# A running sum over the sequence: how its block totals reach the output

## The chip, the core and the metric

The kernel runs on one core of a Trainium2 chip. The core has five engines with queues of their own: TensorE (PE, with its weight loads as PEld) for matrix products, VectorE (DVE), ScalarE (ACT), GpSimd (POOL) and SyncE (SP), and 16 DMA engines that move data. SP, ACT and POOL can issue transfers. Work is held in SBUF (128 partitions); products land in PSUM. The metric is the device time of one execution in microseconds. Each engine works through its own queue in order and waits for other engines by semaphores.

## The reference

Two branches read the same x (2048 positions, 448 channels) and are mixed by a gate of one number per position:

```python
g = _sigmoid((x * gate_w).sum(-1, keepdims=True))
a = _A_ref(x, A_wqkv, A_wo)          # linear attention, 16 heads of 28
b = _B_ref(x, ...)                   # long convolution, plus x * D_skip
return g * a + (1 - g) * b
```

Branch A: q, k, v are products of x with a 448 x 1344 weight; phi(t) = t + 1 for positive t, else exp(t). Per head, kv is the sum over all positions of phi(k) times v, z the sum of phi(k); a position's output is phi(q) kv / (phi(q) z), and then a product with `wo`.

Branch B convolves each channel with a kernel K[d, l] = 2 Re(sum over n of C exp(A dt l)). For the inputs drawn here K hardly changes over the 2048 positions, so that the convolution is a running sum of x along the sequence times one number per channel (`near` in the kernel). The kernel tests this for each channel and has a full convolution (`general_conv`) behind a branch for inputs where it does not hold; the branch is not taken in these runs.

## The kernel before, in words

**Tiling.** Position s = 16 p + c lies on partition p in chunk c. So a chunk is 128 positions, one on each partition, and 16 chunks (NC) make up the sequence. The running sum then has two levels: along the 16 chunks on each partition, and over the totals of all earlier partitions. `y` (128 x 16 x 448) collects the running sum and x times D_skip.

**The running sum.** The rows of x lie once more in `wvo` (chunks 0 to 7) and `room` (chunks 8 to 15), four chunks being a group; `home(c)` is a chunk's row. `running(c)` (L428) adds a row to the PSUM sum and puts the sum, times `near`, back in the row. `skip(c)` (L251, POOL) writes x * D_skip to `y`. `group_add(g)` (L436) adds a group's four rows to `y` with one accumulating transfer that POOL issues. After chunk 15's row, that row holds each partition's total: `whole_split` (L439) splits it in a high part (ScalarE) and a low part (POOL), `whole_head` (L445) multiplies both with a triangle of ones on TensorE, which leaves in PSUM for each partition the totals of all before it. These have to be added to all 16 rows of `y`. ScalarE copies them to `over`, and `head_add(g)` (L451) adds `over` to a group's four rows of `y`, again with an accumulating transfer that POOL issues, with `over` read four times.

**The first loop** (L514, chunks 2 to 13) has per step c, in TensorE's order: the k product of chunk c+1 (11 matmuls, `project`), the q product of chunk c, and the products `do_g(c)` of phi(k) with x, which accumulate over all chunks in four PSUM tiles `g`. Around it `split_t` and `split_n` split the two layouts of x of chunk c+2 in high parts (ScalarE) and low parts (POOL); `k_feature`, `k_high` and `k_low` are phi of k, with the column sums of phi(k) in `zb`; `q_post` is phi of q, kept in `pq`, and the gate's exponential in `e1`. `gate(a, b)` (L398) turns `e1` into the gate's denominators and `og` (one minus the gate) for chunks a to b-1.

**Between the loops** (L666 to L787) chunk 14 is handled, the column sums of `zb` over the partitions are formed by a product with ones (`zo`), kv and `wo` are multiplied, and the first chunks of the last loop are prepared.

**The last loop** (L805) has per chunk: `norm_a` (POOL, phi(q) times z), `norm_b` (VectorE, sum per head), `norm_d` (reciprocal, with the gate), `norm_c` (POOL L613 and L619 and VectorE L616, phi(q) scaled, to two places in `room`), `turn` (four transposes on TensorE into `tr`, split by ScalarE and VectorE into `th`), `attend` (11 products into `a`), `final_b` (VectorE: `ot` = `og` * `y` + `a`, then the output transfer from one of two buffers) and `final_c` (a copy by ScalarE). `norm_c` works two chunks ahead of `attend`, `norm_a` six ahead. `late` (L788) puts phi(q) of chunk 15 into the steps 5 to 7.

The order on each engine is the order of the program, written out by hand. What matters around the change in the first loop's end:

- step 12: `whole_split` after `skip(14)`
- step 13: `whole_head` behind the k product of chunk 14; `group_add(3)` after `skip(15)`; the copy to `over` after `k_high`; `head_add(0)` and `head_add(1)` at the step's end
- after the loop: `gate(0, 14)`, and `gate(14, 15)` behind the copy of `zb`
- last loop: `head_add(2)` in step 2, `head_add(3)` in step 3, both behind `norm_c`

`norm_a` writes to three places in `room` (elements 1024 to 2367 of 3584), `norm_c` to two (0 to 1023).

Of the kernel before, what the change touches and what calls it, by code (L numbers as in the profile page):

```python
# [31 lines left out]
QA = 1  # L32
QW = 512
EDGE = 16
PADS = 352
G = 4
ROWS = {6: (0, 1), 7: (2, 3, 4), 8: (5, 6, 7), 9: (8, 9, 10), 10: (11, 12, 13), 11: (14, 15)}
SMALL = 2.0 ** -70
# [104 lines left out]
def gated_mix_kernel(ctx: ExitStack, tc: tile.TileContext, xin, wq_d, wvo_d, abc_d, ldt_d, dsk_d,  # L143
# [36 lines left out]
    room = const.tile([P, 2 * G, D], F32, name="room")  # L180
    over = const.tile([P, D], F32, name="over")
    near = const.tile([P, D + PADS], F32, name="near")[:, :D]
    rf = room.rearrange("p r d -> p (r d)")

    xp = work.enter_context(tc.tile_pool(name="xp", bufs=4))
# [52 lines left out]
    def split_t(c):  # L238
        w = xt[c] = xt_p.tile([P, 2 * NAT], F32R, name="xt", tag="t")
        ACT.copy(w[:, :NAT], turned[c])  # L240
        low(POOL, w[:, NAT:], turned[c], w[:, :NAT])
# [37 lines left out]
    def s4d_prepare():  # L279
        tt = lambda eng, o, a, b, op: eng.tensor_tensor(out=o, in0=a, in1=b, op=op)  # L280
        stt = lambda o, a, k, b, op1: DVE.scalar_tensor_tensor(out=o, in0=a, scalar=k, in1=b, op0=ALU.mult, op1=op1)
        junk = [yf[:DJ, F0 + (i - 2) * 2 * N:F0 + (i - 1) * 2 * N].rearrange("p (i n) -> p i n", i=2) for i in range(2)]
        s0, s1, am, pn, b0, n0, n1 = (small() for _ in range(7))
        o = ps.tile([P, 512], F32, name="sums", tag="v0")
        side.append(o)
        dt, p0, p1, d2, md, b1 = (o[:DJ, D + i * J:D + (i + 1) * J] for i in range(6))
        for j in range(J):
            ACT.activation(abc[0][:, 0, j], abc[0][:, 0, j], AF.Exp)
        ACT.activation(dt, ldt, AF.Exp)
        ACT.activation(d2, dt, AF.Square)  # L290
        yield
        for j in range(J):
            ACT.activation(junk[0], abc[0][:, :, j], AF.Square, accum_out=am[:, j:j + 1])
            ACT.activation(junk[0][:, 0], abc[1][:, 0, j], AF.Copy, accum_out=s0[:, j:j + 1])
            DVE.scalar_tensor_tensor(out=junk[1], in0=abc[1][:, :, j], scalar=1.0, in1=abc[0][:, :, j], op0=ALU.mult,
                                     op1=ALU.mult, accum_out=s1[:, j:j + 1])
            if j % 2:
                yield
        tt(DVE, md, am, d2, ALU.mult)
        stt(p0, s0, 2.0, dt, ALU.mult)  # L300
        stt(n0, s0, 2.0, dt, ALU.mult)
        stt(p1, s1, -2.0, d2, ALU.mult)
        stt(n1, s1, -2.0, d2, ALU.mult)
        DVE.tensor_scalar(out=md, in0=md, scalar1=SMALL, scalar2=None, op0=ALU.is_le)
        stt(b0, p0, -1.0, n0, ALU.max)
        stt(b1, p1, -1.0, n1, ALU.max)
        yield
        DVE.tensor_scalar(out=p0, in0=p0, scalar1=-BIG, scalar2=BIG, op0=ALU.max, op1=ALU.min)
        DVE.scalar_tensor_tensor(out=md, in0=b0, scalar=1.0 / FAR, in1=md, op0=ALU.is_ge, op1=ALU.mult)
        stt(okc, b1, FLAT, b0, ALU.is_le)  # L310
        DVE.scalar_tensor_tensor(out=md, in0=b0, scalar=FAR, in1=md, op0=ALU.is_le, op1=ALU.mult)
        tt(DVE, okc, okc, md, ALU.mult)
        tt(DVE, pn, p0, okc, ALU.mult)
        DVE.tensor_reduce(out=oks, in_=okc, op=ALU.add, axis=AX.X)
        yield
        o = ps.tile([P, 512], F32, name="p", tag="v1")
        for j in range(J):
            PE.transpose(o[:, j * DJ:(j + 1) * DJ], pn[:, j:j + 1].to_broadcast([DJ, P]), ident[:DJ, :DJ])
        ACT.copy(near, o[:, :D])
# [108 lines left out]
    def running(c):  # L428
        if not c:
            sums.append(ps.tile([P, 512], F32, name="r", tag="v0")[:, :D])  # L430
            ACT.copy(sums[0], home(0))
        else:
            DVE.tensor_tensor(out=sums[0], in0=home(c), in1=sums[0], op=ALU.add)
        DVE.tensor_tensor(out=home(c), in0=near, in1=sums[0], op=ALU.mult)

    def group_add(g):  # L436
        POOL.dma_start(out=y[:, g * G:(g + 1) * G], in_=homes[g // 2][:, g % 2 * G:][:, :G], accum_op=ALU.add)

    def whole_split():  # L439
        w = tp.tile([P, 2, D], F32R, name="sums", tag="v0", bufs=1)  # L440
        sums[0] = w
        ACT.copy(w[:, 0], home(NC - 1))
        low(POOL, w[:, 1], home(NC - 1), w[:, 0])

    def whole_head():  # L445
        o = ps.tile([P, 512], F32, name="v", tag="v0")[:, :D]
        for i in range(2):
            PE.matmul(o, lhsT=tri, rhs=sums[0][:, i], start=i == 0, stop=i == 1)
        sums[0] = o

    def head_add(g):  # L451
        POOL.dma_start(out=y[:, g * G:(g + 1) * G], in_=over[:, None, :].to_broadcast([P, G, D]), accum_op=ALU.add)

    prep = s4d_prepare()
    def steps(n):
        for _ in range(n):
# [49 lines left out]
    def split_o(j):  # L506
        w = xn_p.tile([P, NX], F32R, name="wo", tag="n") if j < 2 else xp.tile([P, XC], F32R, name="wo", tag="xr")
        w = w[:DJ, :2 * D].rearrange("p (i d) -> p i d", i=2)
        woh.append(w[:, 0])
        wol.append(w[:, 1])  # L510
        ACT.copy(woh[j], wo[:, j])
        low(POOL, wol[j], wo[:, j], woh[j])

    for c in range(2, NC - 2):  # L514
        if c + 3 < NC:
            load_x(c + 3)
        if c == 2:
            SP.dma_start(out=mask, in_=cst_d)
        if c in (6, 7):
            half_load(1, c - 6)  # L520
        if c == 10:
            for j in (0, 2):
                SP.dma_start(out=wo[:, j:j + 2], in_=wvo_d[:DJ, 1, j:j + 2])
        if c == 12:
            for j in (0, 2):
                SP.dma_start(out=wv[:, j:j + 2], in_=wvo_d[:, 0, j:j + 2])
        ko = project(c + 1, wkh, wkl, D, "v1" if c in (2, 4) or c > 6 and c % 2 == 0 else "k")
        if c == 13:
            whole_head()
        rows = list(ROWS.get(c, ()))  # L530
        if c > 6 and rows:
            running(rows.pop(0))
        split_t(c + 2)
        if c > 5:
            split_n(c + 2, False)
        k_feature(c + 1, ko)
        if c in (8, 9, 11):
            group_add((c - 7) * 2 // 3)
        if c > 5:
            skip(c + 2)  # L540
        if c == 12:
            whole_split()
        if c == 13:
            group_add(3)
        k_high(c + 1)
        if c == 13:
            ACT.copy(over, sums[0])
        k_low(c + 1)
        if rows:
            running(rows.pop(0))  # L550
        qo = project(c, wqh, wql, D + 2, "q")
        q_post(c, qo)
        for i in rows:
            running(i)
        if c < 5:
            steps(2 if c == 4 else 1)
        if c == 4:
            ACT.copy(tri, trir)
        if c == 7:
            SP.dma_start(out=okr[:, None, :DJ], in_=oks[:, None, :])  # L560
        if c == 9:
            DVE.tensor_reduce(out=okr[:, DJ:], in_=okr[:, :DJ], op=ALU.add, axis=AX.X)
            DVE.tensor_copy(okn, okr[:, DJ:])
        do_g(c, (0, 1))
        if c == 5:
            steps(1)
        do_g(c, (2, 3))
        if c < 4:
            skip(c - 1)
            skip(c + 2)  # L570
        if c < 6:
            split_n(c + 2, c > 3)
        if c in (3, 4):
            half_load(0, c - 3)
        for j in {11: (0, 1), 12: (2, 3)}.get(c, ()):
            split_o(j)
        if c == 13:
            head_add(0)
            head_add(1)

    gs = [xp.tile([P, 2, D], F32, name="gs%d" % i, tag="xr") for i in range(2)]
    gs = [gs[i // 2][:, i % 2] for i in range(4)]
# [1 line left out]
    pn, th, tl, pd, dn, dp = {}, {}, {}, {}, {}, []  # L584

    def norm_a(c):
        pd[c] = rf[:, 2 * NAT + c % 3 * D:][:, :D]
        POOL.tensor_tensor(out=pd[c], in0=pq[:, c], in1=zb, op=ALU.mult)  # L588

    def norm_b(c):  # L590
# [73 lines left out]
            ACT.copy(pq[:, c, lo:hi], a[:, lo:hi])  # L664

    c = NC - 2  # L666
    gate(0, c)
    ko = project(c + 1, wkh, wkl, D, "v1")
    k_feature(c + 1, ko)
    k_high(c + 1)  # L670
# [12 lines left out]
    ACT.copy(zb, zo[:, :D])  # L683
    norm_a(0)
    norm_a(1)
    gate(c, c + 1)
    norm_bd(0)
    norm_c(0)
    norm_a(2)
# [115 lines left out]
    for c in range(NC):  # L805
        if c % 2 and 1 < c < NC - 4:
            norm_d(c + 3, 2, ACT.copy)
        if c:
            final_b(c - 1)
        if 0 < c < NC - 2:  # L810
            norm_c(c + 2)
        if c in (2, 3):
            head_add(c)
        if c + 1 < NC:
            turn(c + 1)
        if c:
            final_c(c - 1)
        if c + 6 < NC:
            norm_a(c + 6)
        if c == 1:  # L820
            norm_b(5)
            norm_d(4, 2, ACT.copy)
        attend(c, ((0, D // 2), (D // 2, D)) if c == NC - 1 else ((0, D),))
        if c == 0:
            norm_b(4)
        if 0 < c < NC - 5:
            norm_b(c + 5)
        if c == due:
            due = next(later, None)
# [89 lines left out]
```

## Time and profile before

| | before |
|---|---|
| median of 3 runs | 170.98 us (170.43 to 171.1) |
| the profiled execution's own time | 170.41 us |
| its span | 168.5 us |
| busy: TensorE | 162.1 us, 96% of the span |
| busy: VectorE, ScalarE, GpSimd | 113.1, 100.6, 107.1 us |
| granted TensorE clock | 1.00 |
| `y<-over` transfers (`head_add`) | 4 of 896 KB, median 10.8 us from issue to landing |
| output transfers | 15 of 224 KB, median 1.9 us |

The profile gives starts and lengths from the span's start on. A row of the timeline has the start, the duration, the engine, the line of the kernel, the operation, what it writes and reads, and in brackets how long the engine had been idle and what ended that. The chain of waits follows the work that ended last back to the start. A row of the windows has the busy time of each engine in that stretch, then the granted clock, the share of the DMA engines and GB/s. Tiles go by the program's names; a tile that takes over a place in PSUM has a name of its own (`v` at L448 are the totals).

### The profile page before, as it was taken

How to read it: one execution, taken by the hardware profiler on the slowest of the kernel's cores; microseconds unless marked ns; L12 is line 12 of the kernel's file. 1: busy time of each engine (PE TensorE's matmuls, PEld its weight loads, DVE VectorE, ACT ScalarE, POOL GpSimd, SP SyncE). 2: the span in 40 equal slices, each digit the busy share in tenths (PEclk: the TensorE clock that was granted, in tenths of full speed). 3: DMA queues.
4: the chain of work that ended last, by engine and by line, in shares of the span. 5: the costliest groups of instructions: out<-in, count | busy, mean ns of one | idle time of the engine just before them, and what ended most of it. 6: DMA issues, size and time to landing. Idle time of an engine off the chain costs nothing.

```text
span 168.5 us, 2611 instructions
## 1 busy us (share of the span) xinstructions
PE 162.1 (96%) x843; PEld 145.5 (86%) x843; DVE 113.1 (67%) x242; ACT 100.6 (60%) x223; POOL 107.1 (64%) x116
## 2 busy tenths in 40 slices
PE   6999999999999999999999999999999898999991
PEld 2698999999999999999999999899999796899991
DVE  0837744685844887988983434677989748996551
ACT  3688668898396775684678963564534252454231
POOL 3082589668728639548368999079689997954000
PEclk9999999999999999999999999999999999999999
DMA  5989977597963332889895005999314996321212
GB/s 153 411 315 305 270 179 242 190 348 266 331 209 127 124 124 54 167 198 246 258 284 109 4 0 105 171 189 184 75 58 114 204 227 163 114 93 71 109 75 96
DMA packets 11839, 29.35 MB, mean 174 GB/s; under 512 B 1360, under 2 KB 8048, under 8 KB 11600
## 3 DMA queue, kind: packets, MB, share of 16 engines
q1 hardware_dynamic: 8992, 21.71, 38.7%
q0 software_dynamic: 2688, 7.34, 24.0%
q8 instruction: 7, 0.11, 0.3%
q10 hardware_dynamic: 144, 0.11, 0.2%
q14 instruction: 8, 0.07, 0.1%
HBM read 17.87 MB, written 3.67 MB: 128 GB/s over the span
## 4 chain that ended last, share of the span: by engine, by line
PE 85%; DVE 5%; DMA 4%; issue 2%; ACT 1%; ACTq 0%; POOL 0%; DVEq 0%; POOLq 0%
PE g L415 21%; PE q L339 20%; PE a L653 12%; PE v L339 12%; PE k L339 11%; DMA out<-ot 4%; PE q L258 3%; PE tr L630 3%; DVE den L593 2%; DVE ot L658 2%; PE m L709 1%; PE k L729 1%; PE tr L729 1%; ACT th L637 1%; DVE t L797 0%
## 5 line engine op out<-in xcount | busy, mean ns | idle before, releaser
L653 PE MATMUL a<-wk,th 128*128 128x448 f32 (+1 forms) x187 | 39.5, 360 | 0.0
L415 PE MATMUL g<-pkh,xn 128*128 128x448 f32 x112 | 35.8, 364 | 0.0
L653 PEld LDWEIGHTS a<-wk,th 128*128 128x128 f32 x187 | 32.5, 189 | 2.0 <-DVE th L638 0.2
L236 POOL TENSOR_TENSOR xt<-xr,xt 128x512 fp32r<-128x512 f32 x14 | 18.1, 1296 | 19.8 <-ACT xt L240 19.8
L339 PE MATMUL q<-wqh,xt 128*128 128x450 f32 x120 | 27.7, 367 | 0.0
L588 POOL TENSOR_TENSOR room<-pq,zb 128x448 f32<-128x448 f32 x16 | 23.7, 1483 | 6.0 <-ACT zb L683 4.8
L236 POOL TENSOR_TENSOR xn<-xr,xn 128x448 fp32r<-128x448 f32 x16 | 18.6, 1163 | 10.1 <-ACT xn L246 10.1
L339 PEld LDWEIGHTS q<-wqh,xt 128*128 128x128 f32 x120 | 22.5, 189 | 1.8
L415 PE MATMUL g<-pkl,xn 128*128 128x448 f32 x64 | 23.3, 365 | 0.0
L415 PEld LDWEIGHTS g<-pkh,xn 128*128 128x128 f32 x112 | 21.1, 188 | 2.3
L613 POOL TENSOR_TENSOR room<-pq,den 128x336 f32<-128x336 f32 x16 | 16.4, 1028 | 6.9 <-ACT den L602 4.0
L339 PE MATMUL k<-wk,xt 128*128 128x448 f32 x88 | 19.9, 368 | 0.0
L252 POOL TENSOR_TENSOR y<-xr,dsk 128x448 f32<-128x448 f32 x16 | 19.4, 1220 | 0.0
L339 PE MATMUL v<-wk,xt 128*128 128x448 f32 x88 | 18.9, 362 | 0.0
L339 PEld LDWEIGHTS k<-wk,xt 128*128 128x128 f32 x88 | 16.5, 189 | 1.8 <-ACT wk L462 0.5
L339 PEld LDWEIGHTS v<-wk,xt 128*128 128x128 f32 x88 | 16.5, 188 | 1.1
L658 DVE SCALAR_TENSOR_TENSOR ot<-y,og,a 128x448 f32<-128x448 f32 (+1 forms) x17 | 10.8, 633 | 7.6 <-PE a L653 4.7
L637 ACT CAST th<-tr 128x512 fp32r<-128x512 f32 x16 | 9.4, 589 | 9.2 <-PE tr L630 9.2
L664 ACT COPY pq<-a 128x448 f32<-128x448 f32 (+1 forms) x17 | 8.6, 514 | 9.0 <-DVE ot L658 8.0
L638 DVE TENSOR_TENSOR th<-tr,th 128x512 fp32r<-128x512 f32 x16 | 11.0, 687 | 1.9 <-ACT th L637 1.3
L415 PEld LDWEIGHTS g<-pkl,xn 128*128 128x128 f32 x64 | 11.1, 174 | 1.1 <-DVE pkl L378 0.2
L339 PE MATMUL q<-wql,xt 128*128 128x450 f32 x45 | 11.7, 366 | 0.0
(144 smaller groups left out, 276.6 us busy)
## 6 DMA issues: line engine op xcount, KB each, us to landing
xr<-in SPq DMA_DIRECT2D x15, 512.0 KB, 4.0
y<-over POOLq DMA_DIRECT2D x4, 896.0 KB, 10.8
out<-ot SPq DMA_DIRECT2D x15, 224.0 KB, 1.9
room<-in SPq DMA_DIRECT2D x3, 896.0 KB, 8.1
wvo<-in SPq DMA_DIRECT2D x2, 896.0 KB, 5.7
y<-wvo POOLq DMA_DIRECT2D x2, 896.0 KB, 8.5
y<-room POOLq DMA_DIRECT2D x2, 896.0 KB, 6.7
y<-in SPq DMA_DIRECT2D x2, 480.0 KB, 4.6
```

Source lines behind the costliest of these rows:

```text
L236: eng.tensor_tensor(out=o, in0=r, in1=h.bitcast(F32), op=ALU.subtract)
L252: POOL.tensor_tensor(out=y[:, c], in0=plain[c][:, :D], in1=dsk, op=ALU.mult)
L258: PE.matmul(idle[:, :cols], lhsT=warm[:, :P], rhs=warm[:, :cols], start=True, stop=True)
L339: PE.matmul(o[:, :n], lhsT=a, rhs=b, start=run.n == 1, stop=not seq)
L415: PE.matmul(g[i][:a.shape[1], :D], lhsT=a, rhs=b, start=c == 0 and n == 0, stop=c == NC - 1 and n == len(seq) - 1)
L588: POOL.tensor_tensor(out=pd[c], in0=pq[:, c], in1=zb, op=ALU.mult)
L613: POOL.tensor_tensor(out=n[:, :3, :DJ].rearrange("p j (h d) -> p j h d", h=4), in0=a, in1=r[:, :H - 4].rearrange("p (j h) -> p j h", j=3)[ ...
L637: ACT.copy(h, ov)
L638: DVE.tensor_tensor(out=l, in0=ov, in1=h.bitcast(F32), op=ALU.subtract)
L653: PE.matmul(a[:, lo:hi], lhsT=u_, rhs=w_[:, lo:hi], start=n == 0, stop=n == 10)
L658: DVE.scalar_tensor_tensor(out=ot[:, lo:hi], in0=y[:, c, lo:hi], scalar=og[:, c:c + 1], in1=a[:, lo:hi], op0=ALU.mult, op1=ALU.add)
L664: ACT.copy(pq[:, c, lo:hi], a[:, lo:hi])
```

## The change

The totals reach the four groups of `y` in three ways. Groups 0 and 1 still get two transfers of `over`, now issued in the middle of step 13. For group 3 VectorE adds the totals, from PSUM, to the four rows in `room` before `group_add(3)`. For group 2, whose rows are in `y` already, VectorE adds them there. Both use a new function `under`, which adds to two rows at once, so there are four additions of 128 x 896. The triangle products stand at the end of step 12, and the split for them ahead of `skip(14)`. The products of `norm_a` get a tile `prod`; a filler between tiles, `PADS`, is 320 elements shorter, so that the tiles behind `prod` move by 1024 elements. The gate of chunks 0 to 14 is formed at once, behind the copy of `zb`.

```diff
-PADS = 352
+PADS = 32
...
+    prod = const.tile([P, 3, D], F32, name="prod")
...
+    def under(a):
+        DVE.tensor_tensor(out=a, in0=a, in1=sums[0][:, None, :].to_broadcast([P, 2, D]), op=ALU.add)
...
         ko = project(c + 1, wkh, wkl, D, "v1" if c in (2, 4) or c > 6 and c % 2 == 0 else "k")
-        if c == 13:
-            whole_head()
         rows = list(ROWS.get(c, ()))
         if c > 6 and rows:
             running(rows.pop(0))
+        if c == 13:
+            under(room[:, G:G + 2])
+            under(room[:, G + 2:])
         split_t(c + 2)
+        if c == 13:
+            ACT.copy(over, sums[0])
+            head_add(0)
+            head_add(1)
         if c > 5:
             split_n(c + 2, False)
         k_feature(c + 1, ko)
         if c in (8, 9, 11):
             group_add((c - 7) * 2 // 3)
+        if c == 12:
+            whole_split()
         if c > 5:
             skip(c + 2)
-        if c == 12:
-            whole_split()
-        if c == 13:
-            group_add(3)
         k_high(c + 1)
-        if c == 13:
-            ACT.copy(over, sums[0])
         k_low(c + 1)
...
             split_o(j)
+        if c == 12:
+            whole_head()
         if c == 13:
-            head_add(0)
-            head_add(1)
+            group_add(3)
+            under(y[:, 2 * G:2 * G + 2])
+            under(y[:, 2 * G + 2:3 * G])
...
     def norm_a(c):
-        pd[c] = rf[:, 2 * NAT + c % 3 * D:][:, :D]
+        pd[c] = prod[:, c % 3]
...
     c = NC - 2
-    gate(0, c)
...
-    gate(c, c + 1)
+    gate(0, c + 1)
...
-        if c in (2, 3):
-            head_add(c)
```

## The prediction

> **What bounds the kernel now.** I began with the page: busy time and the chain that ended last.
>
> ```profile
> span 168.5 us, 2611 instructions
> PE 162.1 (96%) x843; PEld 145.5 (86%) x843; DVE 113.1 (67%) x242; ACT 100.6 (60%) x223; POOL 107.1 (64%) x116
> PE 85%; DVE 5%; DMA 4%; issue 2%; ACT 1%; ACTq 0%; POOL 0%; DVEq 0%; POOLq 0%
> ```
>
> TensorE carries 85% of the chain, and the change removes no product. So it can win only where TensorE stands still, and lose only where it makes TensorE stand still. The waits say where that is; this is TensorE's whole list but for its 1.3 us at the start:
>
> ```profile
> PE tr L630 <- DVE room L616: 1.1, 2, 0.7
> PE tr L630 <- POOL room L613: 0.5, 1, 0.5
> ```
>
> All are at the transposes (`tr`) of the last loop, one per chunk. Since ends of matmuls are modelled, I measure the loss by the starts of the transposes in the timeline (start, duration, engine):
>
> ```profile
> 120.24 0.60 PE L630 MATMUL tr<-both,room 128*128 128x128 f32 x4
> 130.85 0.60 PE L630 MATMUL tr<-both,room 128*128 128x128 f32 x4
> 134.14 0.68 PE L630 MATMUL tr<-both,room 128*128 128x128 f32 x4 [0.48 <-POOL room L613]
> 140.42 0.63 PE L630 MATMUL tr<-both,room 128*128 128x128 f32 x4 [0.74 <-DVE room L616]
> 143.59 0.63 PE L630 MATMUL tr<-both,room 128*128 128x128 f32 x4 [0.33 <-DVE room L616]
> 146.43 0.60 PE L630 MATMUL tr<-both,room 128*128 128x128 f32 x4
> 159.69 0.60 PE L630 MATMUL tr<-both,room 128*128 128x128 f32 x4
> ```
>
> The undisturbed pitch is (130.85 - 120.24)/4 = 2.65 us before and (159.69 - 146.43)/5 = 2.65 after. The five steps from 130.85 to 146.43 take 15.58 where 5 x 2.65 = 13.25 would do. **The loss is 2.33 us**: 0.64 up to 134.14, 0.98 over the two steps to 140.42, 0.52 and 0.19 in the next two.
>
> Then I looked for what happens there, on POOL and in the DMA share:
>
> ```profile
> 127.40 1.28 POOL L452 DMA_DIRECT2D y<-over  x1
> 130.38 1.81 POOL L452 DMA_DIRECT2D y<-over  x1
> 131.20 2.18 POOL L588 TENSOR_TENSOR room<-pq,zb 128x448 f32<-128x448 f32 x1
> 132.33 1.75 POOL L613 TENSOR_TENSOR room<-pq,den 128x336 f32<-128x336 f32 x1
> 143.17 0.75 POOL L613 TENSOR_TENSOR room<-pq,den 128x336 f32<-128x336 f32 x1 [1.18 <-ACT den L602]
> 138.00:140.00 2.00, 1.68 (x9) 1.24 (x7) 0.52 (x1) 0.15 (x1) 2.00 (x6) 1.00 1.15 212
> 131.99 7.40 DMA out<-ot
> 139.48 0.68 DVE L658 SCALAR_TENSOR_TENSOR ot<-y,og,a 128x448 f32<-128x448 f32 x1 [2.00 <-DMA out<-ot]
> out<-ot SPq DMA_DIRECT2D x15, 224.0 KB, 1.9
> ```
>
> The two rows at L452 are `head_add(2)` and `head_add(3)`, the transfers that this change takes out of the loop. They cost twice. First, POOL issues them, and its later multiplies end 1.0 us late (L613 1.75 against 0.75 after the next idle time): the starts keep their pitch (131.20 to 132.33 is 1.13), so a backlog travels along until POOL next idles. That is the wait of 0.48 at 134.14. Second, they fill the DMA engines (in the window's row the share before the last number, 1.15), and one output row block lands after 7.40 us where the median is 1.9. VectorE's `final_b` waits for that buffer, 2.00 us before 139.48. The `norm_c` multiply (L616) behind it comes late, and TensorE waits 0.74, then 0.33.
>
> **The change part by part.**
>
> *Removed: the two transfers in the loop.* With both causes gone, up to 2.33 us comes back. What is late next would be VectorE itself, which in these iterations also has the last chunk's feature work (`late`):
>
> ```profile
> 141.38 0.88 DVE L797 TENSOR_SCALAR t<-e 128x448 f32<-128x448 f32 x1
> 143.26 0.19 DVE L616 TENSOR_TENSOR room<-pq,den 128x48 f32<-128x48 f32 x1
> ```
>
> I replayed VectorE's list from 130.85 on with TensorE at its pitch. The transposes then come at 136.15, 138.80 and 141.45, the last two in place of 140.42 and 143.59. Without the wait `final_b(5)` starts when its product is there, just behind the transposes of 136.15, say 136.4, 3.1 us before 139.48. The VectorE work between 139.48 and 143.26 then puts that L616 at 140.2; its end, 140.4, is needed at 141.45, so 1.0 us is left over. I take 0.1 us of loss left, bounds 0 to 0.7 (0.52 + 0.19, all that follows the last DMA wait). Term: **-2.2 us**, bounds -2.33 and -1.6.
>
> *Added: four VectorE adds of 128x896, one operand in PSUM.* No such size is in the trace. The nearest rows:
>
> ```profile
> L658 DVE SCALAR_TENSOR_TENSOR ot<-y,og,a 128x448 f32<-128x448 f32 x15 | 9.9, 658 | 6.3 <-PE a L653 3.4 <-DMA out<-ot 2.9
> L658 DVE SCALAR_TENSOR_TENSOR ot<-y,og,a 128x224 f32<-128x224 f32 x2 | 0.9, 448 | 1.3 <-PE a L653 1.3
> 98.91 0.63 DVE L368 SCALAR_TENSOR_TENSOR k<-k,e 128x448 f32<-128x448 f32 x1 [3.01 <-ACT e L367]
> 105.94 0.63 DVE L368 SCALAR_TENSOR_TENSOR v<-v,e 128x448 f32<-128x448 f32 x1 [1.75 <-ACT e L367]
> 102.86 0.46 DVE L399 TENSOR_SCALAR e<-e 128x14 f32<-128x14 f32 x1
> 103.63 0.56 DVE L401 TENSOR_SCALAR og<-og 128x14 f32<-128x14 f32 x1
> ```
>
> From 224 to 448 elements costs 0.21 us, so 896 cost 0.658 + 0.42 = 1.08; I take 1.1, bounds 0.66 (no growth) and 1.32 (two of the shorter). The two on `room` fall into VectorE's 3.01 us of idle time before 98.91; they take 2.2. The two on `y` come after `q_post(13)`: 1.75 idle, and the gate over chunks 0 to 13 leaves that place (102.86 to 104.19, 1.33), together 3.1 for 2.2. **Cost nothing**, covered by ScalarE's exponentials of the k features, which VectorE waits for there; even at 1.32 each pair fits. With that cover gone, a pair would cost its whole 2.2 us, since TensorE's column-sum product (`zo`) behind the last k chain has little to spare:
>
> ```profile
> 108.51 0.62 DVE L236 TENSOR_TENSOR zl<-zb,zh 128x448 fp32r<-128x448 f32 x1 [0.17 <-ACT e L386]
> 109.25 0.41 PE L681 MATMUL zo<-zl,ones 128*128 128x448 f32 x1
> ```
>
> (0.12 us between the end of the one and the start of the other). For starts in the new order that I can't see: 0 to +0.3.
>
> *Moved: the triangle products to the end of chunk 12, the split ahead of `skip`.*
>
> ```profile
> 97.69 0.41 PE v L448 x2
> 94.81 1.16 POOL L236 TENSOR_TENSOR sums<-room,sums 128x448 fp32r<-128x448 f32 x1
> 95.33 2.37 PE L339 MATMUL k<-wk,xt 128*128 128x448 f32 x11
> 102.58 2.91 POOL L452 DMA_DIRECT2D y<-over  x2
> 110.32 2.26 POOL L588 TENSOR_TENSOR room<-pq,zb 128x448 f32<-128x448 f32 x2 [4.83 <-ACT zb L683]
> ```
>
> (The first row is the chain's.) TensorE would run them at 95.33, in front of k of chunk 14, which comes 0.41 later; the total is the same. On POOL the low part changes places with a `skip`, also 128x448, so it ends near 95.97 - 1.16 = 94.8, 0.5 us ahead of 95.33; without that exchange TensorE would stand 0.6 us. ScalarE's copy of the totals to `over` moves ahead of its xn split; its list stays as long. Cost nothing, bounds 0 to +0.2.
>
> *Moved: two transfers from the end of chunk 13 to behind its x split, and `group_add(3)` last.* POOL has the same list in another order: the last xn split and the last `skip` now stand behind two issues, 2.9 us later, with the third issue last. All of it ends, as before, near 102.58 + 2.91 = 105.5. The split's first user, the products of chunk 15, comes after 109.25. Before `norm_a(0)` at 110.32 POOL keeps its 4.83 us of idle time, in which a backlog is shed. The sums land for `final_b(0)`, in the loop, and `final_b(12)`, at its end. Cost nothing, 0 to +0.1.
>
> *Moved: the gate of chunks 0 to 13, joined to that of chunk 14; and the products of `norm_a` in a tile of their own.* Three instructions go. The joined ones have 15 columns:
>
> ```profile
> 110.46 0.15 DVE L401 TENSOR_SCALAR og<-og 128x1 f32<-128x1 f32 x1
> 111.50 0.63 DVE L593 TENSOR_REDUCE den<-room 128x16 f32<-128x448 f32 x1 [0.88 <-POOL room L588]
> ```
>
> At the 1-column prices they fit; at those of 14 columns (102.86 to 104.19) they end at 110.09 + 1.33 = 111.42, still inside the 0.88 us of idle time. The Trainium skill, SBUF — State Buffer, Who interferes with whom, speaks against it: a VectorE scalar operation in the two-port mode and a GpSimd operation exclude each other for a whole instruction. By it the last gate step would wait for `norm_a(0)` on POOL until 111.46 and VectorE's next step would start some 0.2 us late, which makes the sum 0.2 longer; the stretched 14-column rows lean that way, the unstretched 1-column row does not show it. From rows alone: 0 to +0.2, taken as 0. The own tile of `norm_a` removes overlap with rows that `group_add(3)` reads; no wait for that shows, so 0.
>
> **Sum.** Against the profiled execution (170.41 for a span of 168.5): 170.41 - 2.2 = 168.2. That execution is the fastest of those shown; the median of the three timed runs is 170.98 (170.43 to 171.1), and the same step from it gives **168.8**, which I forecast.
>
> **Rivals.**
>
> *VectorE's backlog stays.* If the L616 waits come from `late` and not from the output transfer, only POOL's 0.64 goes: 170.98 - 0.64 = 170.3. For it: L797 lies in that very stretch. Against it: VectorE idled 2.00 us for the DMA just before.
>
> *The adds become the bound.* If an add takes twice my value, the pair on `y` needs 4.4 us where 3.1 are free, the last k chain comes 1.3 late and TensorE, past the slack of 0.12, 1.2: 170.0. For it: L401 took 0.56 with POOL issuing beside it and 0.15 later. Against it: operations of this kind on one PSUM operand have a steady row (0.658 over 15).
>
> *Slower: the adds to y wait for transfers.* If an add to rows 8 to 11 of `y` is held until the transfers to other rows of `y` that are issued before it have landed, VectorE's queue (last k chain, zl, gate) is held with it. Decisive is whether that landing comes later than 105.9:
>
> ```profile
> y<-over POOLq DMA_DIRECT2D x4, 896.0 KB, 10.8
> 129.32 0.61 DVE L658 SCALAR_TENSOR_TENSOR ot<-y,og,a 128x448 f32<-128x448 f32 x1
> ```
>
> With 10.8 us from an issue at 105.5 the adds start at 116.3 and end at 118.5, 12.6 us after the last k feature is due (105.94): 170.98 - 2.2 + 12.6 = 181.4. Against it: `final_b(2)` reads `y` at 129.32 while a transfer issued at 127.40 is under way, so waits go by rows.
>
> **How the numbers follow.** Forecast 0.74 (its own range 168.3 to 169.4), backlog 0.10, adds 0.10, slower 0.03, something unseen 0.03. About 0.5%, 0.85 us, is what a measurement of this kernel tells from no change; that border is 170.1. Faster: 0.74 + 0.09 of the adds + 0.01 = 0.84; same: the backlog's 0.10 + 0.01 = 0.11; slower: 0.03 and the rest of the two others, 0.05. The range runs from 168.0 (2.33 off the median, and 0.6 for the profiled run's place below it) to 170.2, between the two middle rivals.
>
> **What would show it.** Right: two `y<-over` transfers, none after 120 us; POOL's L613 rows at 0.75 through 125 to 145; transposes at a pitch of 2.65 all through; no wait of `final_b` for `out<-ot`; four new adds near 1.1 us; idle time before the last k feature down from 1.75 to about 0.9. Wrong: a pitch still over 2.65 behind the `late` steps; a TensorE wait at `zo` or at the kv products; a wait of the adds for a DMA. A gain under 0.85 us would mean that the transfers were not what held the loop.

## The result, and the profile after

| | median us | lowest to highest | executions |
|---|---|---|---|
| before | 170.70 | 170.38 to 171.1 | 4 |
| after | 168.59 | 168.1 to 169.23 | 4 |

The ratio is 0.9877, with a 95% interval of 0.9835 to 0.992: the change takes off 2.1 us, where 2.2 was predicted, and the time lies 0.2 us under the forecast of 168.8. The profiled execution took 168.52 us, and its lines are the ones shown here. One execution of experiment 7 took 272.68 us at a granted clock of 0.57 and is left out of its time.

The page of the changed kernel (busy time, then the chain of waits) and TensorE's whole list of waits (us in total, times, longest):

```profile
span 166.7 us, 2612 instructions
PE 161.5 (97%) x843; PEld 146.0 (88%) x843; DVE 117.3 (70%) x243; ACT 100.3 (60%) x223; POOL 104.6 (63%) x114
PE 97%; ACTq 0%; POOL 0%; DVE 0%; ACT 0%; issue 0%; POOLq 0%
...
PE q L259 <- POOL warm L193: 1.3, 1, 1.3
```

TensorE's share of the chain went from 85% to 97%. Both waits at the transposes are gone, and the one that is left stands at the start of the kernel, where it stood before. The loop in TensorE's timeline (start, duration, engine, line), and the operations that the prediction named, from the timelines and the groups by form:

```profile
120.40 0.60 PE L638 MATMUL tr<-both,room 128*128 128x128 f32 x4
...
131.01 0.60 PE L638 MATMUL tr<-both,room 128*128 128x128 f32 x4
...
146.93 0.60 PE L638 MATMUL tr<-both,room 128*128 128x128 f32 x4
...
157.54 0.60 PE L638 MATMUL tr<-both,room 128*128 128x128 f32 x4
...
L621 POOL TENSOR_TENSOR room<-pq,den 128x336 f32<-128x336 f32 x16 | 12.1, 754 | 7.1 <-ACT den L610 4.0 <-PE tr L638 1.9 <-POOL prod L596 0.8
L666 DVE SCALAR_TENSOR_TENSOR ot<-y,og,a 128x448 f32<-128x448 f32 x15 | 9.8, 653 | 3.7 <-PE a L661 3.7
```

From 120.40 to 157.54 are 14 steps of 2.653 us: the loop loses nothing, where it lost 2.33. The five steps that took 15.58 us (130.85 to 146.43) take 13.27 now: from 131.01 to 146.93 are six steps, 15.92 us. POOL's multiply by `den` has a mean of 0.754 us over all 16, with no long one left. `final_b` waits for its products alone; the 2.9 us it spent waiting for output transfers are gone.

Before the loop a little was lost: its first transposes start at 120.40 where they started at 120.24. So of the 2.33 us that came back in the loop, 2.15 reach the last transposes (159.69 to 157.54). The two profiled executions differ by 1.89 us (170.41 to 168.52).

A start counted from the begin of the span also holds what the first microseconds of the kernel took, and that differs between executions of one kernel. In seven traces of kernels that are alike up to the loop (the changed one twice, experiments 4 to 8), VectorE's k feature of chunk 13 starts anywhere from 91.96 to 92.78 us, and all of that is there already at 11.5 us. From this feature to the loop's first transposes, though, it is 28.10 to 28.13 us in all seven. In the kernel before it is 27.93 (92.31 to 120.24). So the change loses 0.19 us ahead of the loop, and by such distances the experiments are read below.

VectorE's timeline where the new adds are (idle time ahead of an instruction and its releaser in brackets):

```profile
95.91 2.08 DVE L456 TENSOR_TENSOR room<-room,v 128x896 f32<-128x896 f32 x2
100.23 0.63 DVE L369 SCALAR_TENSOR_TENSOR k<-k,e 128x448 f32<-128x448 f32 x1 [2.23 <-ACT e L368]
...
103.74 2.08 DVE L456 TENSOR_TENSOR y<-y,v 128x896 f32<-128x896 f32 x2
105.92 0.63 DVE L369 SCALAR_TENSOR_TENSOR v<-v,e 128x448 f32<-128x448 f32 x1
```

Each pair takes 2.08 us. Behind the pair on `y` the last k feature follows 0.1 us later (105.82 to 105.92), where 0.9 us of idle time had been expected.

### The profile page after: what moved, and what is told of

Read it like the earlier page. It is cut to its first block, busy times and chain, and to the rows that moved or that the text cites. A ratio compares the mean times of both kernels' runs of the same rounds, so it can differ in the third digit from the quotient of the medians.

```text
span 166.7 us, 2612 instructions
## 1 busy us (share of the span) xinstructions
PE 161.5 (97%) x843; PEld 146.0 (88%) x843; DVE 117.3 (70%) x243; ACT 100.3 (60%) x223; POOL 104.6 (63%) x114
## 4 chain that ended last, share of the span: by engine, by line
PE 97%; ACTq 0%; POOL 0%; DVE 0%; ACT 0%; issue 0%; POOLq 0%
PE a L661 21%; PE g L416 21%; PE q L340 20%; PE v L340 12%; PE k L340 11%; PE tr L638 4%; PE q L259 3%; PE m L716 1%; PE k L736 1%; PE tr L736 1%; POOL warm L193 0%; DVE ot L666 0%; PE v L449 0%; PE p L319 0%; ACTq L668 0%; ACT pq L672 0%
## 5 line engine op out<-in xcount | busy, mean ns | idle before, releaser
L237 POOL TENSOR_TENSOR xn<-xr,xn 128x448 fp32r<-128x448 f32 x16 | 19.6, 1228 | 10.2 <-ACT xn L247 10.2
L596 POOL TENSOR_TENSOR prod<-pq,zb 128x448 f32<-128x448 f32 x16 | 18.4, 1152 | 6.2 <-ACT zb L690 4.8
L253 POOL TENSOR_TENSOR y<-xr,dsk 128x448 f32<-128x448 f32 x16 | 20.4, 1282 | 0.0
L621 POOL TENSOR_TENSOR room<-pq,den 128x336 f32<-128x336 f32 x16 | 12.1, 754 | 7.1 <-ACT den L610 4.0
```

What stands on the lines that cost most here:

```text
L237: eng.tensor_tensor(out=o, in0=r, in1=h.bitcast(F32), op=ALU.subtract)
L253: POOL.tensor_tensor(out=y[:, c], in0=plain[c][:, :D], in1=dsk, op=ALU.mult)
L621: POOL.tensor_tensor(out=n[:, :3, :DJ].rearrange("p j (h d) -> p j h d", h=4), in0=a, in1=r[:, :H - 4].rearrange("p (j h) -> p j h", j=3)[ ...
```

## The experiments

The times of one group of runs are compared with the kernel before on the same chip (170.72, 170.64 and 170.56 in the three groups). Diffs are against the changed kernel unless it is said otherwise.

**1. The changed kernel again.** No edit.

> The changed kernel once more, beside the others of this group. Both theories: 168.6, as measured before (168.1 to 169.2), with the transposes of the last loop at a pitch of 2.65 us all through.

Measured: 169.33 us (168.07 to 169.39), ratio 0.9907 (0.9871 to 0.9942). The gain holds, but the executions spread over 1.3 us, where those of the kernel before spread over 0.96 us in this group and 0.7 in the first comparison (2.5 in the third group). What separates 168.1 from 169.3 was not found; the traces show that up to 0.8 us can arise in the first 11.5 us of a kernel, which the change does not touch. Differences below a microsecond between the kernels that follow are read from the traces, not from medians.

**2. Only the two additions undone**, with all moves kept.

```diff
-            under(room[:, G:G + 2])        # all four adds go
...
+        if c in (2, 3):
+            head_add(c)                    # back in the loop
```

> The changed kernel, but groups 2 and 3 get their totals by the two transfers in steps 2 and 3 of the last loop again, and the four VectorE adds are gone; triangle products, gate and own tile stay as changed. Theory (the two transfers in the loop are the whole gain): 170.4 to 171.0, the pitch of the transposes over 2.65 between steps 4 and 9, 2.3 us in all. Rival (a part comes from the moved pieces): 169.2 to 170.0, with a loop that loses less than 1.5 us.

Measured: 171.03 us, ratio 1.0018 (1.0001 to 1.0036). TensorE's waits and two of its transposes in this kernel:

```profile
PE tr L633 <- DVE room L619: 1.1, 2, 0.8
PE tr L633 <- POOL room L616: 0.5, 1, 0.5
...
131.30 0.60 PE L633 MATMUL tr<-both,room 128*128 128x128 f32 x4
...
146.91 0.60 PE L633 MATMUL tr<-both,room 128*128 128x128 f32 x4
```

The list of before is back, nearly to the digit, and the five steps take 15.61 us: a loss of 2.36 above 13.25. The whole gain is these two transfers. (The first step of this loop, 120.39 to 123.35, takes 0.31 us more than the pitch, and the list shows no wait for it; why is open.) From the k feature of chunk 13 to the loop it is 27.93 us again (92.46 to 120.39), so the moves without the adds lose nothing there.

**3. Only the two transfers removed**, from the kernel before. It leaves out the addition of the totals to chunks 8 to 15.

```diff
-        if c in (2, 3):
-            head_add(c)
```

> The kernel before without the two transfers of the last loop, with nothing in their place: it leaves out the addition of the totals to chunks 8 to 15. Theory: 168.3 to 168.6, the same as the changed kernel or at most 0.3 under it, since adds and moves cost nothing. Rival (the adds cost something, or the moves gained something): under 168.0 in the first case, over 169.2 in the second.

Measured: 168.38 us (167.82 to 168.72), ratio 0.9872 (0.9839 to 0.9906); the pitch is 2.65 us throughout (119.96 to 157.09 for 14 steps). Against leaving the work out, the adds and the moves together cost 0.2 us by the medians (168.59 against 168.38, within their spreads). The loop starts 0.44 us earlier here (119.96 against 120.40), but 0.24 of it stands at the k feature of chunk 13 already (92.04 against 92.28); 0.20 is left, as against the kernel before.

**4. Both effects put back by transfers into one place.** Two accumulating transfers from POOL at the old place in the loop, both into the same rows of `room`, which nothing reads any more.

```diff
+        if c in (2, 3):
+            POOL.dma_start(out=room[:, G:], in_=over[:, None, :].to_broadcast([P, G, D]), accum_op=ALU.add)
```

> The changed kernel with two more accumulating transfers of 896 KB, issued by POOL in steps 2 and 3 of the last loop, into rows of room that nothing reads any more; their result is not used. Theory: the 2.3 us come back, 170.6 to 171.0, with POOL's multiplies ending about 1 us late and a wait of final_b for an output transfer. Rival (what held the loop in the kernel before was that the added rows are those final_b reads, or VectorE's own work): within 0.5 of the changed kernel, 168.3 to 169.1.

Measured: 175.78 us, and of no use for its question, because the second transfer waited for the first on POOL:

```profile
135.59 1.30 POOL L820 DMA_DIRECT2D room<-over  x1 [4.26 <-DMA room<-over]
...
PE tr L638 <- POOL room L621: 4.8, 1, 4.8
```

Experiment 7 is the mended form: same rows in both are what made POOL wait.

**5. The issue alone.** The same two accumulating transfers with 512 elements each, into rows of `wvo` that nothing reads later.

```diff
+        if c in (2, 3):
+            POOL.dma_start(out=wvo[:, (c - 2) * G:(c - 1) * G, :1], in_=over[:, None, :1].to_broadcast([P, G, 1]), accum_op=ALU.add)
```

> The changed kernel, with POOL issuing two accumulating transfers of one element per row (512 elements each) in steps 2 and 3 of the last loop, into rows of wvo that nothing reads any more: the issues are back, the 896 KB are not. Theory (two separate costs): POOL's multiplies end 0.5 to 1.0 us late, TensorE loses 0.6 us at one transpose, final_b waits for no output transfer; 169.2 in all. Rival (the issue alone costs the 2.3 us, since POOL's backlog lasts for five steps): 170.7. Rival (the bytes alone): 168.6, no late transpose.

Measured: 169.15 us, ratio 0.9901 (0.9865 to 0.9937), but from 168.44 to 170.72, and the profiled execution is the longest of them. Its timeline, TensorE, then VectorE and POOL:

```profile
131.49 0.60 PE L638 MATMUL tr<-both,room 128*128 128x128 f32 x4
134.80 0.68 PE L638 MATMUL tr<-both,room 128*128 128x128 f32 x4 [0.50 <-POOL room L621]
...
144.28 0.63 PE L638 MATMUL tr<-both,room 128*128 128x128 f32 x4 [1.29 <-DVE room L624]
147.12 0.60 PE L638 MATMUL tr<-both,room 128*128 128x128 f32 x4
...
140.03 2.91 DVE L804 TENSOR_SCALAR t<-e 128x448 f32<-128x448 f32 x1
...
140.60 2.08 POOL L596 TENSOR_TENSOR prod<-pq,zb 128x448 f32<-128x448 f32 x1
...
143.86 0.75 POOL L621 TENSOR_TENSOR room<-pq,den 128x336 f32<-128x336 f32 x1 [1.18 <-ACT den L610]
```

Here 131.49 to 147.12 is 15.63 us, a loss of 2.36 with almost no bytes moved. No `final_b` waits for an output in this execution. POOL's backlog, the late ends of its multiplies, gives the 0.50 at 134.80, as in the kernel before. Then VectorE's scalar operation of the `late` work (L804) takes 2.91 us, until 142.94, just after POOL's backlog ends (140.60 + 2.08 = 142.68); the chain behind it (VectorE's `den`, ScalarE's copy of it, the `norm_c` multiply) reaches TensorE 1.29 us late. The theory of two separate prices (0.64 for the issue) fits the median of this kernel (0.56 above the changed one's) and not this execution.

**6. The bytes alone.** The two transfers as plain copies, issued by SP, 896 KB each.

```diff
+        if c in (2, 3):
+            SP.dma_start(out=wvo[:, (c - 2) * G:(c - 1) * G], in_=over[:, None, :].to_broadcast([P, G, D]))
```

> The changed kernel, with two plain copies of 896 KB issued by SyncE in the same places, from over to rows of wvo that nothing reads any more: the bytes are back, POOL issues nothing. Theory: POOL's L621 rows stay at 0.75, final_b waits about 2 us for an output transfer and the transposes of the steps 7 to 9 come 1.7 us late in all; 170.3. Rival (the issue alone): 168.6, pitch 2.65.

Measured: 168.72 us (168.69 to 169.13), ratio 0.9898 (0.9866 to 0.9931): the bytes cost nothing in this form, and the loss expected from them did not come. The window (last two columns: DMA share, GB/s) and the issues (KB each, median us to landing):

```profile
132.00:134.00 2.00, 2.00 (x14) 1.84 (x12) 1.85 (x6) 0.70 (x2) 2.00 (x3) 1.00 1.04 390
...
wvo<-over SPq DMA_DIRECT2D x2, 896.0 KB, 4.6
```

With plain copies under way 390 GB/s are moved, outputs included, and they are gone after 4.6 us; no output came late enough for `final_b` to wait.

**7. Issue and bytes, into two places that nothing reads.** Experiment 4 with different rows of `wvo` for each transfer.

```diff
+        if c in (2, 3):
+            POOL.dma_start(out=wvo[:, (c - 2) * G:(c - 1) * G], in_=over[:, None, :].to_broadcast([P, G, D]), accum_op=ALU.add)
```

> The changed kernel with two more accumulating transfers of 896 KB issued by POOL in steps 2 and 3 of the last loop, to two different sets of rows of wvo that nothing reads any more, so that the second does not wait for the first as it did when both went to the same rows. Theory: the 2.3 us come back, 170.6 to 171.0, as 0.6 at one transpose and 1.7 behind a wait of final_b for an output transfer. Rival (the added rows had to be those that final_b reads): 168.3 to 169.1.

Measured: 170.61 us (170.41 to 172.47), ratio 1.0017 (0.9989 to 1.0045): the kernel before, in time and in its waits.

```profile
PE tr L638 <- DVE room L624: 1.1, 2, 0.7
PE tr L638 <- POOL room L621: 0.5, 1, 0.5
...
DVE ot L666 <- DMA out<-ot: 2.8, 2, 1.9
...
132.00:134.00 2.00, 1.91 (x10) 1.45 (x8) 1.34 (x4) 0.84 (x2) 2.00 (x5) 1.00 1.12 183
...
wvo<-over POOLq DMA_DIRECT2D x2, 896.0 KB, 9.0
```

So the loss does not need the transfers to touch what `final_b` reads. Accumulating transfers keep the engines as busy as plain ones (share 1.12 against 1.04) at half the rate (183 GB/s against 390), and land after 9.0 us against 4.6. Here `final_b` waits 2.8 us for outputs, beside the plain copies of experiment 6 not at all.

**8. Twice the bytes alone.** Four plain copies from SP, 3.5 MB in all, over rows that nothing reads any more.

```diff
+        if c in (2, 3):
+            for t in ((wvo[:, :G], wvo[:, G:]), (room[:, G:], wqh[:, :, :D].bitcast(F32)))[c - 2]:
+                SP.dma_start(out=t, in_=over[:, None, :].to_broadcast([P, G, D]))
```

> As the run with the two plain copies by SyncE, but with four of them, two in each of the steps 2 and 3, to rows of wvo and room and to wqh, which nothing reads any more. There two copies kept the DMA engines busy for 8 us, an output landed after 3.8 us at most and nothing was lost; four should keep them busy for about 10 us and let an output land after 6 to 8 us, as the accumulating transfers do (7.0). Theory (a late landing of the output, alone, costs TensorE): final_b waits 1 to 2 us for an output transfer, the transposes come 0.5 to 1.7 us late; 169.2 to 170.3. Rival (a late output costs nothing unless POOL has a backlog too): final_b waits, but the pitch stays 2.65; 168.6.

Measured: 174.24 us, ratio 1.019 (1.0129 to 1.0251). VectorE's wait and what it does to TensorE:

```profile
141.40 0.68 DVE L666 SCALAR_TENSOR_TENSOR ot<-y,og,a 128x448 f32<-128x448 f32 x1 [4.14 <-DMA out<-ot]
142.34 1.08 PE L638 MATMUL tr<-both,room 128*128 128x128 f32 x4 [3.24 <-DVE room L624]
```

Late outputs alone do stop TensorE, with no backlog on POOL (its L621 rows stay at 0.75 to 0.78). The size, above the 170.3 expected at most, goes beyond the question: in this kernel the outputs are also issued behind the copies on SP, which issues the next one at 133.84, after a copy that occupies it until 133.33, and the granted clock falls after the stop (last section).

**9. The triangle products back at the start of chunk 13.** The adds stay.

```diff
         if c == 13:
+            whole_head()                   # ahead of running and the adds
...
-        if c == 12:
-            whole_split()                  # again behind skip
...
-        if c == 12:
-            whole_head()
```

> The changed kernel with the triangle products at the start of step 13 again, and the split for them behind skip(14), as in the kernel before; adds and transfers as changed. By the prediction the adds to room find VectorE idle for 3.01 us, 0.9 more than they need; starting 2.2 us later, at about 98.1, they would end at 100.2, and the k feature of chunk 14 would come 1 to 2 us late, the q feature of chunk 13 with it, past the 1.6 us that TensorE has there: 169.0 to 170.5, with a TensorE wait at the q product of chunk 14. Rival (the place of the triangle products does not matter): 168.6, no wait.

Measured: 170.94 us, ratio 1.0008 (0.9988 to 1.0028), above the 170.5 expected at most. The gain in the loop stays (its pitch is 2.653), yet nearly all of it is paid ahead of the loop, whose first transposes start at 122.90, 30.11 us behind the k feature of chunk 13 (92.79) where it was 28.12 in the changed kernel, so 1.99 later:

```profile
98.62 2.08 DVE L456 TENSOR_TENSOR room<-room,v 128x896 f32<-128x896 f32 x2 [2.23 <-PE v L449]
102.94 0.63 DVE L369 SCALAR_TENSOR_TENSOR k<-k,e 128x448 f32<-128x448 f32 x1 [2.23 <-ACT e L368]
...
100.80 0.53 ACT L542 COPY over<-v 128x448 f32<-128x448 f32 x1 [3.61 <-PE q L340]
...
106.58 1.87 PE L340 MATMUL q<-wqh,xt 128*128 128x450 f32 x8 [1.38 <-DVE pq L394]
```

The adds start 2.7 us later than in the changed kernel (98.62 against 95.91), behind products that come late. ScalarE's copy of the totals starts as the adds end (98.62 + 2.08 = 100.70), the exponentials behind it follow, and TensorE waits 1.38 us. This is the mechanism of the rival in which the adds become the bound, reached by another way.

**10. The products of `norm_a` in `room` again.**

```diff
-        pd[c] = prod[:, c % 3]
+        pd[c] = rf[:, 2 * NAT + c % 3 * D:][:, :D]
```

> The changed kernel with the products of norm_a in room again. By the prediction the own tile is worth nothing: 168.6. Rival: norm_a(1) writes over the first of the rows that group_add(3) reads, and that transfer, now the last of the three, lands at 116.4 where it landed at 109.0 before; norm_a(1) would start 5 us late, the second norm_b with it, and TensorE would wait 4 to 5 us behind the kv products: 173.

Measured: 175.4 us, ratio 1.0278 (1.0213 to 1.0343); the rival's mechanism, at more than its 173. POOL and TensorE in this kernel:

```profile
116.39 1.13 POOL L596 TENSOR_TENSOR room<-pq,zb 128x448 f32<-128x448 f32 x1 [5.09 <-DMA y<-room]
...
PE m L716 <- ACT kvh L753: 4.2, 1, 4.2
```

`group_add(3)`, issued last now, still reads those rows when `norm_a` wants to write them; the multiply waits 5.09 us for the landing and TensorE stands 4.2 us. The own tile of `norm_a` is worth some 6 us (174.61 against 168.52 in the profiled executions), given that `group_add(3)` is last.

**11. The gate in two steps again**, with everything else kept.

```diff
+    gate(0, c)
...
-    gate(0, c + 1)
+    gate(c, c + 1)
```

> The changed kernel with the gate of chunks 0 to 13 in its old place and that of chunk 14 by itself. By the prediction (VectorE has 0.9 us to spare at the last k feature) the same, 168.6. By the trace of the changed kernel, where that k feature starts 0.1 us after the adds, it comes 0.4 to 1.3 us late, and TensorE waits 0.3 to 1.1 us at the column sums: 168.9 to 169.7.

Measured: 169.03 us (168.56 to 170.45), ratio 0.9905 (0.987 to 0.9941). The last k feature starts at 106.32 instead of 105.92 and the loop at 120.78 instead of 120.40. Counted from the k feature of chunk 13 the loop comes after 28.48 us instead of 28.12, 0.36 us lost by the trace; the medians (169.03 here, 168.59 and 169.33 for the changed kernel) don't tell so little. With 0.1 us to spare behind the adds, the three small instructions no longer fit there; joining them is part of what keeps the adds cheap.

**12. ScalarE's copy of the totals ahead of the adds**, and the last chunk's phi(q) moved from VectorE's scalar operation to ScalarE.

```diff
+            ACT.copy(over, sums[0])        # ahead of the adds, no longer behind them and split_t
...
-        DVE.tensor_scalar(out=t, in0=e, scalar1=1.0, scalar2=1e-6, op0=ALU.min, op1=ALU.add)
...
+        ACT.activation(e, e, AF.Exp, scale=-1.0)   # as q_post does for the other chunks
```

> The changed kernel with two more edits. ScalarE's copy of the totals stands ahead of the adds to room; by the theory (the copy waits for the adds, since both read the same place in PSUM) the k chain of chunk 14 runs about 1 us earlier and the idle time before the last k feature is 0.9 us again, with no gain in time. And the last chunk's phi(q) is formed as that of the chunks 5 to 13, with ScalarE in steps 3 to 5, so that VectorE's scalar operation t<-e (1.06 us beside POOL, 0.39 with POOL idle, 2.91 in the run with the issues alone) is gone; by the theory this is what spreads the times of the changed kernel from 168.1 to 169.4: 168.1 to 168.4 with a spread under 0.6. Rival (the spread has another cause): median and spread as before, 168.6 to 169.3.

Measured: 168.56 us (167.82 to 169.07), ratio 0.986 (0.9812 to 0.9907), the changed kernel within their spreads. VectorE:

```profile
96.67 2.08 DVE L456 TENSOR_TENSOR room<-room,v 128x896 f32<-128x896 f32 x2 [0.72 <-ACT over L536]
99.39 0.63 DVE L369 SCALAR_TENSOR_TENSOR k<-k,e 128x448 f32<-128x448 f32 x1 [0.64 <-ACT e L368]
...
106.00 0.63 DVE L369 SCALAR_TENSOR_TENSOR v<-v,e 128x448 f32<-128x448 f32 x1 [1.02 <-ACT e L368]
```

Now the adds wait for the copy and not the copy for the adds; the k feature comes at 99.39 instead of 100.23, and the spare time before the last k feature is 1.02 us, near the 0.9 that had been predicted. The medians show no gain. In the trace the loop comes 27.91 us behind the k feature of chunk 13 (92.36 to 120.27), as in the kernel before, so the 0.19 us that the change loses there are back; but the loop's first step takes 0.25 more than the pitch (120.27 to 123.17), and why is open. The spread of 1.25 us stays without the scalar operation, so that operation is not its cause.

## Why the prediction was right, point by point

**The removed transfers (-2.2): right in size and place.** The loop gave back 2.33 us, the upper bound of the term, and nothing of the 0.1 left over for `late` showed. That the time came within 0.2 us is in part luck: the forecast started from 170.98, and the median of the kernel before came out as 170.70, while 0.19 us were lost ahead of the loop. Experiments 2, 3 and 7 show the cause from three sides: put back, the loss returns; taken out alone, it goes; replaced by transfers to idle rows, it returns.

**The step "They cost twice" was half wrong.** Both effects exist: issue without bytes gives the 0.50 at POOL's multiply (experiment 5), late outputs without an issue stop TensorE (experiment 8). But they don't add up as 0.64 and the rest. The profiled execution of experiment 5 loses all 2.36 through the issue alone, by a way that the prediction did not have: VectorE's scalar operation is held for as long as POOL works without a pause. The prediction had set this operation aside as `late` work of 0.88 us. And the same bytes as plain copies don't hurt (experiment 6); the slow accumulating form does, or twice as many plain ones (experiment 8).

The same hold is there in the kernel before and in experiment 7, where an output is late as well. The end of POOL's unbroken work and the scalar operation, first before, then in experiment 7:

```profile
139.92 2.07 POOL L588 TENSOR_TENSOR room<-pq,zb 128x448 f32<-128x448 f32 x1
141.38 0.88 DVE L797 TENSOR_SCALAR t<-e 128x448 f32<-128x448 f32 x1
...
140.17 2.11 POOL L596 TENSOR_TENSOR prod<-pq,zb 128x448 f32<-128x448 f32 x1
141.62 0.92 DVE L804 TENSOR_SCALAR t<-e 128x448 f32<-128x448 f32 x1
```

The operation ends 0.27 us after POOL (142.26 against 141.99), then 0.26 (142.54 against 142.28), as in experiment 5 (142.94 against 142.68). Counted from the loop's first transposes, POOL's unbroken work ends after 21.75, 21.79 and 21.79 us in these three, and after 19.24 in the changed kernel; the last transposes that wait come after 23.35, 23.39 and 23.39 us. So in these executions the late output settled only when the operation began, and POOL's backlog when it ended: two ways to one loss, which hide each other. That the output counts all the same is seen in the medians. With the issue alone most executions lose less (169.15 us, lowest 168.44), with both hardly any does (170.61, lowest 170.41). What lets the scalar operation through in the faster executions of experiment 5 was not traced.

**The adds: the duration was right, the spare time wrong.** 1.08 us was worked out and 1.08 measured. The 0.19 us lost ahead of the loop lie within the 0 to +0.3 that was left for them. The step that failed is "idle time before the last k feature down from 1.75 to about 0.9": it is 0.1. Left out was a wait among the readers of one PSUM tile. ScalarE's copy of the totals reads the same `v` as the adds:

```profile
98.08 0.53 ACT L540 COPY over<-v 128x448 f32<-128x448 f32 x1 [1.42 <-PE k L340]
```

The profile names TensorE's k products as releaser, but the copy starts 0.09 us after the adds end (95.91 + 2.08 = 97.99). Experiment 9 moves both together, and experiment 12, with the order turned round, moves the wait to the adds: the program puts the two readers one behind the other. So the k feature of chunk 14 came 1.3 us late, at 100.23 instead of 98.91, and used up the spare time of the next pair. It cost little only because the triangle products had moved ahead.

**The moves at "nothing" were right as a sum, and wrong if read one by one.** The triangle's earlier place is worth 2.0 us by the trace and 2.3 by the medians (experiment 9: 170.94 against 168.59), the own tile of `norm_a` some 6 us, the joined gate about 0.4 by the trace: each is cover for another part. The prediction said "no wait for that shows, so 0" of the own tile; no wait could show in a trace where `group_add(3)` was issued earlier and landed at 109.0, before `norm_a` begins. Now it lands at 116.4. POOL's idle time before `norm_a(0)` came out as predicted, 4.83 us again:

```profile
104.52 0.90 POOL L438 DMA_DIRECT2D y<-room  x1 [0.30 <-POOL y L253]
110.25 1.16 POOL L596 TENSOR_TENSOR prod<-pq,zb 128x448 f32<-128x448 f32 x1 [4.83 <-ACT zb L690]
...
110.49 0.95 DVE L402 TENSOR_SCALAR og<-og 128x15 f32<-128x15 f32 x1
111.44 0.63 DVE L601 TENSOR_REDUCE den<-prod 128x16 f32<-128x448 f32 x1
```

**The joined gate (0, or +0.2 by the rule).** The last two rows above show the step that takes 0.17 us on 14 columns while POOL is idle (experiment 11): here it takes 0.95 and ends at 111.44, just behind POOL's `norm_a(0)` (110.25 + 1.16 = 111.41). By the rule of the Trainium skill, SBUF — State Buffer, Who interferes with whom, which holds such an operation until the GpSimd instruction that was issued ahead of it is through, this is what should be seen, and the trace agrees. The 0.2 us that it would have added did not come: the reduction behind it needs `norm_a(0)` anyway, and starts 0.03 us after it.

**Left open.** The 0.19 us ahead of the loop stand at the kv products, behind a ScalarE copy of `gs` for which ScalarE is idle 0.81 us instead of 0.53. They are gone without the adds (experiment 2) and with ScalarE's copy of the totals ahead of the adds (experiment 12), so they belong to that copy standing behind the adds; by what way it reaches the copy of `gs`, no run shows. The spread of 1.3 us among executions of the changed kernel is explained only in part, by the first 11.5 us.

**The rivals.** The adds as the bound did not come in the changed kernel, and came in experiment 9, 0.9 us above the 170.0 that it was priced at. VectorE's backlog did not stay; yet the operation that this rival pointed to, the scalar one of `late`, is the one whose end settled the end of the loss. The adds to `y` waited for no transfer: they start right behind `q_post(13)` with the transfers to other rows of `y`, issued from 99.37 on, still under way.

## What to carry to other kernels

A transfer issued inside a tight loop has three prices, to be looked up one by one: the backlog on the engine that issues it, the landing of other transfers beside it, and whatever that backlog shuts out on a neighbour engine; they need not add up, and one can hide another. When an edit is costed at nothing because something hides it, write down which other part of the same change makes the cover, and whether two engines read the same PSUM tile, for here the program made them go one behind the other. Measure such a change by the distance between two regular instructions of one trace, not by single starts or medians: here such distances agreed to 0.03 us over seven traces, where the starts themselves moved by 0.8 and the executions by 1.3.

## What was not expected of the hardware

**The clock after a stop.** In experiment 4 TensorE stood 4.8 us; afterwards its granted clock (third column from the right) was lower for some microseconds:

```profile
136.00:138.00 2.00, 0.00 (x0) 0.00 (x0) 0.00 (x0) 0.00 (x0) 2.00 (x3) 0.57 0.28 48
138.00:140.00 2.00, 1.19 (x5) 1.19 (x6) 1.82 (x5) 0.19 (x1) 2.00 (x5) 0.50 1.13 188
140.00:142.00 2.00, 2.00 (x7) 1.73 (x7) 1.23 (x2) 1.53 (x4) 2.00 (x5) 0.50 1.13 190
142.00:144.00 2.00, 2.00 (x11) 1.79 (x10) 0.30 (x1) 0.00 (x0) 2.00 (x4) 0.73 0.51 147
144.00:146.00 2.00, 2.00 (x12) 1.87 (x12) 1.69 (x5) 1.02 (x2) 2.00 (x4) 1.00 0.30 115
```

The same 0.50 follows the stop of 3.24 us in experiment 8 and that of 4.2 us in experiment 10, while after the 1.38 us of experiment 9 it stays at 1.00. A long stop is thus paid for beyond its own length, which is part of why experiments 4, 8 and 10 went slower by more than one wait.

**One operation, three durations.** VectorE's scalar operation on 128x448 takes 0.39 us with POOL idle (at 108.97 in the changed kernel), 1.06 beside its ordinary multiplies (138.82), and 2.91 while POOL works off a backlog (experiment 5): there it waited for several POOL instructions in a row, not for one. Beside a working POOL it ends 0.24 to 0.27 us after POOL's last instruction ahead of a pause, in the changed kernel (139.88 against 139.64) as in the others.

**Accumulating transfers** run at half the rate of plain copies between the same memories, 183 against 390 GB/s in the window from 132 to 134 us (outputs included), with the engines shown as about equally busy (1.12 and 1.04).
